# An order planner that lets VectorE's two-input operations run beside POOL's, and scalings of probabilities on POOL

## The chip, the cores and the metric

The kernel runs on one core of one Trainium2 chip. A core has a matrix engine (TensorE, PE in the profile; its weight loads are PEld), three engines for elementwise work (VectorE or DVE, ScalarE or ACT, GpSimd or POOL), and SyncE (SP), which issues all DMAs of this kernel. The matrix engine writes to an accumulator memory, PSUM; operands lie in SBUF. The metric is the device time of one execution in microseconds (us), the median of several runs.

## The reference

Windowed attention with a distance bias, followed by a gated feed-forward network (FFN), all in float32.

```python
# q, k, v: (8 batches, 8 heads, 576 tokens, 64)
scores = q @ k.T / 8 - slope[h] * (i - j)       # for 0 <= i - j < 128, else -1e9
attn   = exp(scores - max); attn = attn / (sum(attn) + 1e-9)
x      = (attn @ v), heads side by side         # (4608, 512)
out    = (sigmoid(x @ w_gate) * (x @ w_val)) @ w_out   # d_ff = 1536
```

The weights arrive as 64-bit floats and the output is float32.

## The kernel before

**Attention.** The 64 pairs of batch and head are worked as 32 units of two heads, each of nine blocks of 128 queries. PE makes the scores of eight blocks at a time (line 416); DVE copies masked halves over each other (428) and adds the bias and takes the row extreme (436); ACT takes the exponential and its row sum (439). Three blocks make a group: DVE adds 1e-9 to the three sums (454), takes the reciprocals (456), and each block is scaled by its reciprocal (`args` in `probabilities`, on ACT at line 459 or on DVE at 460). PE transposes the group (464), a copy brings it to SBUF (187 on ACT, 188 on DVE), and POOL writes it twice, masked, into the layout that the product with V needs (475). PE multiplies with V (501).

**First FFN part.** While the attention runs, PE also multiplies the finished tokens of the first 3072 with four of the twelve column blocks of the two weight matrices (553). Each float32 operand is split into a high part (a copy to a rounded type, lines 187 and 188) and a low part (the operand minus its high part, `minus`, lines 195 on POOL and 196 on DVE), and three products stand for one. Weights are turned from 64-bit to 32-bit floats by integer operations (`decode`, lines 312, 313 and 316).

**Second FFN part and the output.** The tokens lie in five groups. For each group seven combinations of its inputs are made (`add` in `ffn2`, line 650) and split; for every column block PE makes seven products (687), and DVE and ACT combine them and form the gate (694, 698, 702). The result goes to DRAM and comes back for the last product (817), again from seven combinations (`add` in `last`, line 772).

**What sets the order.** Nothing above is issued in the order in which the program states it. Each operation is put into a graph with an engine, a cost in us, its reads and writes, and a wanted time; some have further `ways`, on other engines with other costs. `Graph.order` plans all of it as a list: at each step it takes, over all operations whose inputs are planned and over all their ways, the one with the smallest start plus cost beyond the operation's cheapest way (plus 0.1 us for a way on DVE that isn't the first); ties go to the earlier wanted time. An operation starts when its engine is free, its inputs are there and, if the way counts as `shared`, when the one `port` is free; it then holds that port for its cost:

```python
s = max(free[e], o.ready, port if shared else 0.0)
key = (s + cost - least + (YIELD[e] if k else 0.0), o.want, o.seq)
...
if shared:
    port = o.start + o.cost
```

All POOL ways are shared; DVE's are where `port=True` or the third entry of a way says so. The instructions are then issued to each engine in the planned order, and semaphores keep them right whatever their real durations are. The plan thus sets two things: which engine does an operation that has several ways, and in which order each engine does its work.

Of the kernel before, what the change touches and what calls it, by code (L numbers as in the profile page):

```python
# [12 lines left out]
ALU = mybir.AluOpType  # L13
# [143 lines left out]
def dve_cost(n, psum=False, two=False):  # L157
    return 0.07 + n * (0.00104 if psum or two else 0.00053)
# [7 lines left out]
def attention_gated_ffn(ctx: ExitStack, tc: tile.TileContext, qd, kd, vd, wg, wv, wo, out):  # L166
    nc = tc.nc
    ctx.enter_context(tc.manual_schedule())
    g = Graph()
# [24 lines left out]
    def minus(out, a, b, n, reads, writes, want, psum=False, pool=True):  # L194
        way = ("POOL", 0.1 + n * 0.00223, True, lambda: nc.gpsimd.tensor_tensor(out(), a(), b(), op=ALU.subtract))
        g.add("DVE", dve_cost(n, psum, True), lambda: nc.vector.tensor_tensor(out(), a(), b(), op=ALU.subtract),  # L196
              reads, writes, want, port=not psum, ways=[way] if pool and not psum else [])

    ident = const.tile([P, P], F32, name="ident")
    make_identity(nc, ident)  # L200
# [102 lines left out]
    def decode(src, fc, bits, kb, want, release=0.0):  # L303
        s = raws[0] % NRAW
        raws[0] += 1
        kr = ("wraw", s)
        if src.dtype == F32:
            move(lambda: as32(bits()), lambda: src[fc], [], [kb], want, 256, False, release)
            return
        raw = lambda: T(moe, f"wraw{s}", [P, DM, 2], I32)  # L310
        move(lambda: raw().rearrange("p f t -> p (f t)"), lambda: src[fc].bitcast(I32), [], [kr], want, 512, True, release)
        g.add("ACT", act_cost(DM), lambda: nc.scalar.mul(as32(bits()), as32(raw()[:, :, 1]), 2.0 ** -112), [kr], [kb], want)
        g.add("DVE", dve_cost(DM), lambda: nc.vector.tensor_scalar(
            bits(), bits(), 3, None, op0=ALU.logical_shift_left), [], [kb], want, port=True)
        for word, scalar, o0 in ((0, 29, ALU.logical_shift_right), (1, -0x80000000, ALU.bitwise_and)):
            g.add("DVE", dve_cost(DM, two=True), lambda word=word, scalar=scalar, o0=o0: nc.vector.scalar_tensor_tensor(  # L316
                bits(), raw()[:, :, word], scalar, bits(), op0=o0, op1=ALU.bitwise_or), [kr], [kb], want, port=True)

    def parts(hi, lo, val, n, reads, k0, k1, want):
        copy(hi, val, n, reads, [k0], want)  # L320
# [127 lines left out]
    def probabilities(u, i0):  # L448
        m, _, st, pb, kst, kpb = three_of(u, i0)
        want = u.when(i0 + TRI)  # L450
        slack = 0.0 if u.n < HEAD else SLACK
        n, kb = TRI, ("both", m % NBOTH)
        both = lambda: spread2[m % NBOTH]
        g.add("DVE", 0.07, lambda: nc.vector.tensor_scalar_add(st()[:, 6:9], st()[:, 3:6], 1.0e-9),
              [(kst, 3 + e) for e in range(n)], [(kst, 6)], want)
        g.add("DVE", 0.09, lambda: nc.vector.reciprocal(st()[:, 6:9], st()[:, 6:9]), [], [(kst, 6)], want)
        for e in range(n):
            args = lambda e=e: (pb()[:, e], pb()[:, e], st()[:, 6 + e:7 + e])
            g.add("ACT", 0.3, lambda args=args: nc.scalar.mul(*args()), [(kst, 6)], [(kpb, e)], want,  # L459
                  ways=[("DVE", 0.16, True, lambda args=args: nc.vector.tensor_scalar_mul(*args()))])  # L460

        def transpose():
            for e in range(n):
                nc.tensor.transpose(tp[:, e], pb()[:, e], ident)  # L464

        g.add("PE", 0.11 * n + 0.1, transpose, [(kpb, e) for e in range(n)], [TP], want, slack=slack)
        copy(lambda: both(), lambda: tp[:, 0:n], n * P, [TP], [kb], want, psum=True)
        for own in range(2):
            step, cmp, mult = ([1, P], ALU.is_ge, -1) if own else ([-1, P], ALU.is_gt, 1)

            def spread(own=own, step=step, cmp=cmp, mult=mult):
                f0 = 2 * i0 + own
                nc.gpsimd.affine_select(pt(u)[:, f0:f0 + 2 * n - 1:2, :], both(), [[0, n], step], cmp, 0.0,  # L475
                                        base=0, channel_multiplier=mult)

            g.add("POOL", 0.13 + 0.12 * n, spread, [kb], [("pt", u.n % NPT, i0 + e, own) for e in range(n)], want)
# [155 lines left out]
    def ffn2(t, w, todo, F, ends=False):  # L634
# [13 lines left out]
        def add(o, a, b, op, reads, writes):  # L648
            way = ("POOL", 0.1 + m * 0.00223, True, lambda: nc.gpsimd.tensor_tensor(o(), a(), b(), op=op))
            g.add("DVE", dve_cost(m, two=True), lambda: nc.vector.tensor_tensor(o(), a(), b(), op=op), reads + ["w2pool"], writes, F,  # L650
                  port=True, ways=[way])

        if not made:
            for h in range(2):
                a = t0 + h * N2
                while a < t0 + (h + 1) * N2:
                    b = a // S
                    e = min((b + 1) * S, t0 + (h + 1) * N2)
# [3 lines left out]
                    a = e  # L662
# [12 lines left out]
        def chunk(i, fc):  # L675
            bx, by, bz = bank(), bank(), bank()
            e = turns[0] % (4 if ends else 2)
            turns[0] += 1
            a1, u2, p5, v5 = lambda: low()[:, 2], lambda: low()[:, 3], lambda: hs(e)[:, 1, 0:N2], lambda: hs(e)[:, 0, 0:N2]
            sg = [lambda h=h: T(moe, f"sg{h}", [P, NB], F32)[:, 0:N2] for h in range(2)]  # L680
            bk = lambda b: (lambda: mm[b][:, 0:N2])

            def product(k, b, start, wk):
                def six():
                    for c in range(2):
                        for j, (xp, wp) in enumerate(((0, 0), (0, 1), (1, 0))):
                            nc.tensor.matmul(mm[b][:, 0:N2], w.tile2(i, wp)[:, wk, c * P:(c + 1) * P], combo(k, xp, N2)[:, c],  # L687
                                             start=(start and c == 0 and j == 0), stop=(c == 1 and j == 2), skip_group_check=True)
                wa = 0 if wk < 2 else 2
                g.add("PE", 6 * (N2 / 2400 + 0.0133), six, [("ar", k, 0), ("ar", k, 1), ("w2", i, 0, wa), ("w2", i, 1, wa), "seam"],  # L690
                      [("mm", b)], 1.0e6)

            def total(o, b, a, reads, writes, okeys):
                g.add("DVE", dve_cost(N2, psum=True), lambda: nc.vector.tensor_tensor(o(), bk(b)(), a(), op=ALU.add),  # L694
                      [("mm", b), *reads] if okeys else reads, writes, F)

            def gate(b, h):
                g.add("ACT", act_cost(N2, psum=True), lambda: nc.scalar.activation(sg[h](), bk(b)(), AF.Tanh, scale=0.5),  # L698
                      [("mm", b)], [("sg", h)], F)

            def gated(o, val, reads, writes, h, psum):
                g.add("DVE", dve_cost(N2, psum, True), lambda: nc.vector.scalar_tensor_tensor(  # L702
                    o(), sg[h](), 1.0, val(), op0=ALU.add, op1=ALU.mult), [("sg", h), *reads], writes, F, port=not psum)

            ka, ku, kp, kv = "a1", "u2", ("hs", e, 1), ("hs", e, 0)
            product(0, bx, True, 0)
            copy(a1, bk(bx), N2, [("mm", bx)], [ka], F, psum=True)
            product(3, bz, True, 3)
            copy(p5, bk(bz), N2, [("mm", bz)], [kp], F, psum=True)
            product(4, bx, False, 4)  # L710
            copy(u2, bk(bx), N2, [("mm", bx)], [ku], F, psum=True)
            product(1, by, True, 1)
            total(bk(by), by, a1, [ka], [("mm", by)], False)
            gate(by, 0)
            product(5, bx, False, 5)
            total(p5, bx, p5, [], [kp], True)
            product(2, bz, False, 2)
            total(bk(bz), bz, u2, [ku], [("mm", bz)], False)
            gated(v5, bk(bz), [("mm", bz)], [kv], 0, True)
            product(6, bx, False, 6)  # L720
            gate(bx, 1)
            gated(p5, p5, [], [kp], 1, False)
            c, q, m = place(fc)
            move(lambda: hid[c, q, t][m].rearrange("p (h t) -> p h t", h=2), lambda: hs(e)[:, :, 0:N2], [kp, kv], [("hid", fc, t, 0)], F, N2, True)
# [32 lines left out]
    def last(t):  # L757
        F = FIRST + 2
        t0, N2 = GROUPS[t]
        n = 2 * N2  # L760
# [8 lines left out]

        def add(o, a, b, op, reads, writes):  # L770
            way = ("POOL", 0.1 + n * 0.00223, True, lambda: nc.gpsimd.tensor_tensor(o(), a(), b(), op=op))
            g.add("DVE", dve_cost(n, two=True), lambda: nc.vector.tensor_tensor(o(), a(), b(), op=op), reads, writes, F, port=True, ways=[way])

        bks = [[bank() for _ in range(3)] for _ in range(2)]
        bk = lambda b: (lambda: mm[b][:, 0:N2])
# [14 lines left out]
        for k in ORDER:  # L790
# [19 lines left out]
            for j in range(2):  # L810
                bx, by, bz = bks[j]
                b = {0: bx, 3: bz, 4: bx, 1: by, 5: bx, 2: bz, 6: bx}[k]
# [179 lines left out]
```

## Time and profile before

| | |
|---|---|
| median of 3 runs | 1001.75 us (999.0 to 1001.84) |
| the profiled execution | 1000.32 us, span 998.6 us |
| PE busy | 977.3 us (98%) |
| DVE busy | 771.5 us (77%) |
| ACT busy | 525.1 us (53%) |
| POOL busy | 124.5 us (12%), 217 instructions |

The span is the time from the first to the last instruction. A row of a group of instructions names the line, the engine, the operation, the tiles written and read, the shape and the count; then the busy time in us, the mean in ns, and the idle time just before with what ended it. A row of one line's instructions has least, median and most in ns. A row of a stretch begins with its bounds and length, then has the busy time of each engine (PE, PEld, DVE, ACT, POOL) with its count, and at the end the granted clock, the share of the DMA engines and GB/s; for one line's instructions it has only that line's engine.

### The profile page before, as it was taken

The page shows a single profiled execution, that of the slowest core. Times are in us where ns is not written, and L with a number is a line of the kernel's source. Part 1 is how long each engine was busy: PE and PEld are TensorE (multiplying, and loading weights), DVE is VectorE, ACT ScalarE, POOL GpSimd, SP SyncE. Part 2 cuts the span into 40 slices and gives each one's busy share as a digit, 9 for nine tenths or more (in the row PEclk, how much of TensorE's full clock was granted, in tenths as well). Part 3 has the DMA queues.
Part 4 walks back from the last instruction along what each step waited for, and adds up shares of the span by engine and source line. Part 5 has one row for each costly group of instructions (what it writes and reads, how often), then busy time and mean ns, then how long its engine had stood idle before and what let it go on. Part 6 is the DMA issues. An engine that isn't in the chain of part 4 may idle for free.

```text
span 998.6 us, 17735 instructions
## 1 busy us (share of the span) xinstructions
PE 977.3 (98%) x6202; PEld 843.6 (84%) x6202; DVE 771.5 (77%) x1951; ACT 525.1 (53%) x1350; POOL 124.5 (12%) x217
## 2 busy tenths in 40 slices
PE   8799899999999999999999999999999999999998
PEld 7577677778888999999988888888888888889998
DVE  7998968977866979966895596494479877878783
ACT  4999778768774546535354263362344433333341
POOL 1334543423331100000010000000000000000000
PEclk9899999999999999999999999999999999999999
DMA  7677866875724444332656265439885536162601
GB/s 271 219 259 251 325 225 219 293 233 181 235 93 169 145 148 132 132 137 90 221 203 233 113 209 223 169 116 366 282 307 156 184 99 208 58 194 80 190 16 64
DMA packets 82074, 185.98 MB, mean 186 GB/s; under 512 B 7744, under 2 KB 36800, under 8 KB 81984
## 3 DMA queue, kind: packets, MB, share of 16 engines
q1 hardware_dynamic: 81984, 184.84, 53.9%
q8 instruction: 49, 0.80, 0.3%
q14 instruction: 41, 0.34, 0.1%
HBM read 122.95 MB, written 61.87 MB: 185 GB/s over the span
## 4 chain that ended last, share of the span: by engine, by line
PE 87%; ACT 5%; DVE 5%; DMA 2%; issue 1%; POOL 0%; ACTq 0%; POOLq 0%; DVEq 0%
PE mm L687 39%; PE mm L817 25%; PE mm L553 10%; PE mm L501 5%; PE mm L416 4%; PE mm L464 3%; ACT pb L439 2%; DMA hid<-later_hs 1%; ACT pb L459 1%; PE mm L258 1%; DMA rows_h<-hid 1%; DVE mm L428 1%; ACT early_xr L187 1%; DVE wbits L316 0%; DMA kr<-in_k_dram 0%
## 5 line engine op out<-in xcount | busy, mean ns | idle before, releaser
L687 PE MATMUL mm<-xc,w2s 128*128 128x384 f32 (+1 forms) x2016 | 404.1, 362 | 0.1
L687 PEld LDWEIGHTS mm<-xc,w2s 128*128 128x128 f32 x2016 | 363.8, 188 | 40.3 <-DVE xc L196 0.5
L817 PE MATMUL mm<-duo,wo 128*128 128x512 f32 (+1 forms) x1260 | 259.2, 367 | 0.2 <-DVE duo L196 0.2
L817 PEld LDWEIGHTS mm<-duo,wo 128*128 128x128 f32 x1260 | 229.2, 188 | 30.2 <-DVE duo L196 0.6
L553 PE MATMUL mm<-first,first 128*128 128x512 f32 x576 | 156.1, 409 | 1.8 <-DVE first L196 1.8
L553 PEld LDWEIGHTS mm<-first,first 128*128 128x128 f32 x576 | 103.2, 191 | 25.0 <-issue 4.2
L694 DVE TENSOR_TENSOR mm<-mm,low 128x384 f32<-128x384 f32 (+1 forms) x96 | 60.3, 629 | 72.3 <-PE mm L687 72.1
L698 ACT ACTIVATE sg<-mm 128x384 f32<-128x384 f32 (+1 forms) x96 | 52.0, 544 | 117.9 <-PE mm L687 71.9
L439 ACT ACTIVATE pb<-pb,st 128x128 f32<-128x128 f32 x216 | 84.5, 397 | 8.4 <-DVE st L436 8.2
L187 ACT COPY low<-mm 128x512 f32<-128x512 f32 (+1 forms) x93 | 49.6, 534 | 71.3 <-PE mm L687 65.1
L501 PEld LDWEIGHTS mm<-pt,vr 128*64 128x64 f32 x832 | 61.4, 137 | 12.0 <-issue 8.6
L501 PE MATMUL mm<-pt,vr 128*64 128x256 f32 (+2 forms) x832 | 66.9, 306 | 0.0
L475 POOL TENSOR_SCALAR_AFFINE_SELECT pt<-early_h 128x384 f32<-128x384 f32 x96 | 53.1, 576 | 93.1 <-ACT early_h L187 90.7
L475 POOL TENSOR_SCALAR_AFFINE_SELECT pt<-early_xr 128x384 f32<-128x384 f32 x96 | 50.2, 546 | 100.7 <-ACT early_xr L187 91.3
L428 DVE COPY_PREDICATED mm<-early_h,mm 128x256 f32<-128x256 int32 (+1 forms) x144 | 48.8, 391 | 11.1 <-PE mm L416 10.7
L436 DVE CUSTOM_DVE_ANT_0 pb<-mm,early_h 128x128 f32<-128x128 f32 x216 | 51.0, 281 | 0.0
L464 PE MATMUL mm<-ident,pb 128*128 128x128 f32 x216 | 38.6, 287 | 11.2 <-ACT early_xr L187 7.2
L464 PEld LDWEIGHTS mm<-ident,pb 128*128 128x128 f32 x216 | 25.0, 142 | 23.9 <-ACT early_xr L187 9.7
L187 ACT COPY early_xr<-mm 128x384 f32<-128x384 f32 (+2 forms) x72 | 31.5, 460 | 21.1 <-PE mm L464 13.0
L439 ACT ACTIVATION_READ_ACCUMULATOR pb<-pb,st 128x1 f32 x216 | 41.8, 193 | 0.0
L694 DVE TENSOR_TENSOR later_hs<-mm,later_hs 128x384 f32<-128x384 f32 (+1 forms) x48 | 29.8, 620 | 14.2 <-PE mm L687 6.0
L702 DVE SCALAR_TENSOR_TENSOR later_hs<-sg,later_hs 128x384 f32<-128x384 f32 (+1 forms) x48 | 29.8, 621 | 12.5 <-ACT sg L698 12.5
(133 smaller groups left out, 1181.3 us busy)
## 6 DMA issues: line engine op xcount, KB each, us to landing
hid<-later_hs SPq DMA_DIRECT2D x24, 512.0 KB, 4.1
wo<-stash_o SPq DMA_DIRECT2D x12, 896.0 KB, 7.4
vr<-in_v_dram SPq DMA_DIRECT2D x32, 288.0 KB, 3.2
hid<-later_hs SPq DMA_DIRECT2D x24, 384.0 KB, 2.9
stash_o<-wtmp SPq DMA_DIRECT2D x12, 768.0 KB, 4.3
wraw<-in_moe_w_gate_dram SPq DMA_DIRECT2D x16, 512.0 KB, 4.9
wraw<-in_moe_w_val_dram SPq DMA_DIRECT2D x16, 512.0 KB, 4.7
kr<-in_k_dram SPq DMA_DIRECT2D x11, 576.0 KB, 6.0
```

Of the source, the lines that this page charges most:

```text
L187: g.add("ACT", act_cost(n, psum), lambda: nc.scalar.copy(out(), src()), reads, writes, want, release=release, ways=[("DVE", dve_cost(n, ps ...
L428: g.add("DVE", dve_cost((a1 - a0) * P, psum=True), lambda b=b, a0=a0, a1=a1: nc.vector.copy_predicated(quads(b)[:, a0:a1, 1:3], before[:, ...
L436: g.add("DVE", 0.21, lambda: nc.vector.tensor_tensor_reduce(pb()[:, e], sp[b][:, a, D:D + P], relm[u.p][:, w], op0=ALU.add, op1=ALU.min, s ...
L439: g.add("ACT", 0.39, lambda: nc.scalar.activation(pb()[:, e], pb()[:, e], AF.Exp, bias=st()[:, e:e + 1], scale=-1.0, accum_out=st()[:, 3 + ...
L464: nc.tensor.transpose(tp[:, e], pb()[:, e], ident)
L475: nc.gpsimd.affine_select(pt(u)[:, f0:f0 + 2 * n - 1:2, :], both(), [[0, n], step], cmp, 0.0, base=0, channel_multiplier=mult)
L501: nc.tensor.matmul(to()[e * D:(e + 1) * D, a - e * S - t0:b - e * S - t0], vraw(u)[:, c], seen, start=first, stop=last, skip_group_check=True)
L553: nc.tensor.matmul(mm[s][:, 0:wd], w.tile(kind, wi, i)[:, c * P:(c + 1) * P], xpart(x, c)[:, 0:wd], start=(k == 0 and c == 0), stop=(k == ...
L687: nc.tensor.matmul(mm[b][:, 0:N2], w.tile2(i, wp)[:, wk, c * P:(c + 1) * P], combo(k, xp, N2)[:, c], start=(start and c == 0 and j == 0), ...
L694: g.add("DVE", dve_cost(N2, psum=True), lambda: nc.vector.tensor_tensor(o(), bk(b)(), a(), op=ALU.add), [("mm", b), *reads] if okeys else ...
L698: g.add("ACT", act_cost(N2, psum=True), lambda: nc.scalar.activation(sg[h](), bk(b)(), AF.Tanh, scale=0.5), [("mm", b)], [("sg", h)], F)
L817: nc.tensor.matmul(mm[b][:, 0:N2], wo2(2 * q + m, wp)[:, k, j * P:(j + 1) * P], duo(xp)[:, m], start=(k in (0, 3, 1) and q == 0 and m == 0 ...
```

## The change

Operations of DVE with two inputs (`tensor_tensor`, `scalar_tensor_tensor`) lose their hold on the port in the plan: the subtractions of `minus`, the two integer merges of `decode`, the additions of `ffn2` and `last`, and the gate on SBUF operands. DVE's operations that keep it are the plain copies, the shift of `decode`, the scalings, and, newly, the addition of 1e-9. The scaling gets a third way, on POOL, as a multiplication by the reciprocal and then by 1.0. Two costs are set anew: 0.1 for 0.07 and 0.196 for 0.16 us.

```diff
     def minus(out, a, b, n, reads, writes, want, psum=False, pool=True):
         way = ("POOL", 0.1 + n * 0.00223, True, lambda: nc.gpsimd.tensor_tensor(out(), a(), b(), op=ALU.subtract))
         g.add("DVE", dve_cost(n, psum, True), lambda: nc.vector.tensor_tensor(out(), a(), b(), op=ALU.subtract),
-              reads, writes, want, port=not psum, ways=[way] if pool and not psum else [])
+              reads, writes, want, ways=[way] if pool and not psum else [])
...
             g.add("DVE", dve_cost(DM, two=True), lambda word=word, scalar=scalar, o0=o0: nc.vector.scalar_tensor_tensor(
-                bits(), raw()[:, :, word], scalar, bits(), op0=o0, op1=ALU.bitwise_or), [kr], [kb], want, port=True)
+                bits(), raw()[:, :, word], scalar, bits(), op0=o0, op1=ALU.bitwise_or), [kr], [kb], want)
...
-        g.add("DVE", 0.07, lambda: nc.vector.tensor_scalar_add(st()[:, 6:9], st()[:, 3:6], 1.0e-9),
-              [(kst, 3 + e) for e in range(n)], [(kst, 6)], want)
+        g.add("DVE", 0.1, lambda: nc.vector.tensor_scalar_add(st()[:, 6:9], st()[:, 3:6], 1.0e-9),
+              [(kst, 3 + e) for e in range(n)], [(kst, 6)], want, port=True)
...
             g.add("ACT", 0.3, lambda args=args: nc.scalar.mul(*args()), [(kst, 6)], [(kpb, e)], want,
-                  ways=[("DVE", 0.16, True, lambda args=args: nc.vector.tensor_scalar_mul(*args()))])
+                  ways=[("DVE", 0.196, True, lambda args=args: nc.vector.tensor_scalar_mul(*args())),
+                        ("POOL", 0.3, True, lambda args=args: nc.gpsimd.tensor_scalar(*args(), 1.0, op0=ALU.mult, op1=ALU.mult))])
...
             g.add("DVE", dve_cost(m, two=True), lambda: nc.vector.tensor_tensor(o(), a(), b(), op=op), reads + ["w2pool"], writes, F,
-                  port=True, ways=[way])
+                  ways=[way])
...
                 g.add("DVE", dve_cost(N2, psum, True), lambda: nc.vector.scalar_tensor_tensor(
-                    o(), sg[h](), 1.0, val(), op0=ALU.add, op1=ALU.mult), [("sg", h), *reads], writes, F, port=not psum)
+                    o(), sg[h](), 1.0, val(), op0=ALU.add, op1=ALU.mult), [("sg", h), *reads], writes, F)
...
-            g.add("DVE", dve_cost(n, two=True), lambda: nc.vector.tensor_tensor(o(), a(), b(), op=op), reads, writes, F, port=True, ways=[way])
+            g.add("DVE", dve_cost(n, two=True), lambda: nc.vector.tensor_tensor(o(), a(), b(), op=op), reads, writes, F, ways=[way])
```

## The prediction

> **What bounds the kernel now.** I read the page's slices first, then a table of engine time by stretch, then the chain of waits, and last the rows of the operations that the change touches. The page:
>
> ```profile
> span 998.6 us, 17735 instructions
> PE   8799899999999999999999999999999999999998
> DVE  7998968977866979966895596494479877878783
> ACT  4999778768774546535354263362344433333341
> POOL 1334543423331100000010000000000000000000
> ```
>
> Each digit is a slice of 25 us. PE is short of full only in the first five slices and the last; POOL is idle for most of the run. The table of stretches (length, then busy us of PE, weight load, DVE, ACT, POOL, each with its count) says how much:
>
> ```profile
> 0.00:20.00 20.00, 17.47 (x165) 15.14 (x169) 14.34 (x85) 9.90 (x39) 2.88 (x11) 1.00 0.79 281
> 20.00:120.00 100.00, 87.00 (x926) 66.79 (x919) 91.50 (x457) 89.42 (x351) 40.09 (x68) 0.96 0.75 254
> 120.00:320.00 200.00, 198.06 (x1793) 159.28 (x1793) 153.08 (x718) 144.36 (x526) 67.96 (x125) 0.99 0.62 208
> 340.00:600.00 260.00, 260.00 (x1375) 243.72 (x1374) 206.08 (x335) 121.45 (x215) 10.64 (x10) 1.00 0.47 165
> 600.00:998.60 398.60, 394.92 (x1859) 341.13 (x1857) 287.00 (x331) 148.41 (x203) 2.07 (x2) 1.00 0.50 169
> ```
>
> From 120 us on PE has work almost without a break: 1.94 us idle in 120 to 320, none in 340 to 600, 3.68 in the rest. Nothing that relieves DVE or ACT there can shorten the run. From 20 to 120 PE is idle 13.0 us while DVE is busy 91.5% and ACT 89.4%: there the two elementwise engines hold the attention back. The chain of waits, cut at 119 us, agrees:
>
> ```profile
> by line: ACT pb L439 17.0%; PE mm L501 10.2%; PE mm L553 7.1%; PE mm L416 6.7%; PE mm L464 6.1%; ACT pb L459 6.0%; DVE mm L428 5.4%; DVE wbits L316 4.1%; ACT early_xr L187 4.0%; ACT early_h L187 3.7%; issue 3.3%; ACT wbits L312 3.1%; DVE fi
> by line: PE mm L553 46.4%; PE mm L501 20.2%; PE mm L416 14.4%; PE mm L464 11.4%; DMA kr<-in_k_dram 2.5%; ACT pb L439 1.2%; ACT pb L459 0.7%; DVE first L196 0.7%; issue 0.6%; ACT tt L312 0.6%; ACT early_xr L187 0.5%; DVE tt L316 0.3%; ACT sg
> ```
>
> The first row is 20 to 119 us: PE's four lines hold 30.1%, issue 3.3%; with some 5% for what the cut row hides, about 62% lies with ACT and DVE. The second row is 119 to 318 us: PE holds 92%. So the change can gain in the front 100 us alone, and at most about the 13 us of idle PE there; and it can lose wherever a PE that is full now comes to wait.
>
> **Part 1: scalings may go to POOL.** There are 288 scalings (96 groups of three). By stretch, first on ACT (line 459), then on DVE (line 460):
>
> ```profile
> 20.00:120.00 100.00, 21.86 (x65) 0.96 0.75 254
> 20.00:120.00 100.00, 10.51 (x40) 0.96 0.75 254
> L475 POOL TENSOR_SCALAR_AFFINE_SELECT pt<-early_xr x96: 514/521/1207, 14.0 to 302.7; 128x384 f32<-128x384 f32 x96
> masks.py:199 POOL TENSOR_SCALAR_AFFINE_SELECT ident<-ident x1: 292/292/292, 1.1 to 1.1; 128x128 f32<-128x128 f32 x1
> L195 POOL TENSOR_TENSOR tt<-tt x8: 732/768/1597, 177.3 to 550.4; 128x256 f32<-128x256 f32 x8
> ```
>
> No scaling has run on POOL. Its nearest row is the mask of one 128x128 tile, 292 ns, also one input of the same size; I take 0.3 us. The other end is the shortest two-input operation, 732 ns for 256 elements.
>
> How many go there is the planner's choice. It takes the earliest of start plus cost beyond the cheapest way: 0.104 us for ACT and for POOL, 0.1 for DVE. An exponential on ACT has no such penalty, so on a busy ACT the exponentials go first and the scaling finds POOL, idle 60 of those 100 us. I take two thirds of the 105, 70 operations; the ends are none and all. Two thirds of 21.86 us is 14.6 off ACT, of 10.51 is 7.0 off DVE. The planner can shift copies between these two, so each gets 10.8 us less work; 62% of that is on the chain: **-6.7 us** (0 to -10). From 120 us on the same move is worth nothing, because PE's work covers it; were that cover gone, another 23.8 us on each engine would count.
>
> What stands behind a moved scaling: POOL works in order, so the mask operations (line 475) queue behind it, and the product with V waits for these. POOL's load there rises from 40.1 to about 61 us, so the queue is short and I add nothing; at the long end of 0.73 us it would be 91 us, and the gain of this part would be gone. No DMA is moved past anything: all DMAs are SP's, POOL issues none.
>
> **Part 2: subtractions and additions with two inputs in SBUF may be planned beside POOL.** In the old plan they hold the shared port, so POOL's own version is seldom the earlier one. Without that, it is chosen whenever DVE is booked further ahead than the difference in cost. In the front stretch line 196 has this much:
>
> ```profile
> 20.00:120.00 100.00, 10.86 (x17) 0.96 0.75 254
> ```
>
> A quarter moved is 2.7 us off DVE, half of it after the balance with ACT, 62% of that: **-0.8 us** (0 to -3).
>
> **Part 3: what POOL and DVE cost each other.** The plan now says nothing. The trace does not. Three pairs, first in the front, then twice in the later stages (start, us; the row of line 650 has ns, least, median and most):
>
> ```profile
> 110.22 2.92 POOL L195 TENSOR_TENSOR w2s<-tt,w2s 128x1280 fp32r<-128x1280 f32 x1
> 112.19 0.98 DVE L454 TENSOR_SCALAR st<-st 128x3 f32<-128x3 f32 x1
> 482.43 0.73 POOL L195 TENSOR_TENSOR tt<-tt 128x256 f32<-128x256 f32 x1 [139.19 <-DVE tt L196]
> 482.67 1.57 DVE L650 TENSOR_TENSOR low<-later_xr 128x1024 f32<-128x1024 f32 x1
> L650 DVE TENSOR_TENSOR later_xr<-later_xr x6: 946/1084/1220, 323.3 to 604.9; 128x768 f32<-128x768 f32 x3, 128x1024 f32<-128x1024 f32 x3
> 340.17 1.05 DVE L196 TENSOR_TENSOR w2s<-wbits,w2s 128x512 fp32r<-128x512 f32 x1
> 341.78 1.45 POOL L195 TENSOR_TENSOR tt<-wbits,tt 128x256 f32<-128x256 f32 x1
> ```
>
> The addition at 482.67 took 1.57 us; the longest of the same line and width in the row below it took 1.22. POOL's operation ended 0.49 us after the addition began (482.43 + 0.73 = 483.16), and 0.35 of that is in its time. POOL in turn took 1.45 instead of 0.73 us at 341.78. So a two-input operation of DVE and one of POOL do not overlap here: they take turns.
>
> The Trainium skill, page "SBUF — State Buffer", section "Who interferes with whom", states this rule: a DVE instruction with two SBUF inputs contends with a GpSimd instruction that reads SBUF, and the second to issue waits until the first has ended. The three pairs agree. By it, each of the 70 moved scalings can cost DVE its whole 0.3 us, and the sum at the end of this part would be +0.5 us in place of -3.8.
>
> How often does it strike? The mask operation's median is 521 ns, and the small DVE operation of line 454 gives the DVE side:
>
> ```profile
> L454 DVE TENSOR_SCALAR st<-st x96: 137/168/978, 10.9 to 292.5; 128x3 f32<-128x3 f32 x96
> L454 DVE TENSOR_SCALAR st<-st 128x3 f32<-128x3 f32 x96 | 20.4, 212 | 14.6 <-ACT pb L439 10.2 <-ACT early_xr L439 2.2 <-ACT early_h L439 1.8
> ```
>
> Mean less median is 44 ns, 4.2 us over 96 operations, or 0.02 us for each of some 210 operations of POOL. That is the low end, since the old plan kept the two apart; the high end is the whole 0.3. I take 0.1 us for each of 70: 7 us of DVE, 3.5 after the balance, 62% of it: **+2.2 us** (0.4 to 6.5). That line 454 itself is now planned apart from POOL can win back at most those 4.2 us over the run, a third of them in the front: under 0.5, taken as nothing, as are the two new cost figures for the planner.
>
> **Part 4: the later stages.** Between two token groups of the second FFN stage DVE must make the next inputs (lines 196 and 650), and there it is full:
>
> ```profile
> 330.00:430.00 100.00, 99.87 (x573) 99.01 (x572) 92.24 (x163) 51.78 (x96) 3.31 (x3) 1.00 0.43 143
> 500.00:530.00 30.00, 30.00 (x144) 26.03 (x143) 28.63 (x38) 17.25 (x26) 4.60 (x4) 1.00 0.68 246
> 650.00:670.00 20.00, 20.00 (x89) 16.54 (x89) 19.35 (x26) 14.11 (x21) 1.27 (x2) 1.00 0.20 72
> 747.00:998.60 251.60, 247.92 (x1211) 219.80 (x1210) 195.69 (x209) 90.25 (x113) 0.00 (x0) 1.00 0.40 127
> L687 PEld LDWEIGHTS mm<-xc,w2s 128*128 128x128 f32 x2016 | 363.8, 188 | 40.3 <-DVE xc L196 0.5
> ```
>
> PE already waited 0.5 us for such an input, so the slack is small. Where two or more such operations are queued, the new plan gives some to POOL. Two rows of POOL (732 ns for 256, 2.92 us for 1280) make 2.1 ns an element, so 2.4 us for 1024 elements, against 1.2 on DVE, and meanwhile DVE's other two-input work stands. I expect about 3 per handover, six handovers with the first; operations on PSUM fill most of the lost time. **+1.5 us** (-0.5 to +12, the upper end worked out under the third rival).
>
> **Sum:** -6.7 - 0.8 + 2.2 + 1.5 = **-3.8 us**. The profiled execution took 1000.32 us, 1.7 beyond its span, and would become 996.5. It lies 1.4 below the median of 1001.75; on the median's scale the forecast is **998 us**.
>
> **The rivals.** Three runs of this kernel spread over 0.28%, so 0.3% (3 us) is what a measurement can tell from no change.
>
> *The forecast, 998 us.* For it: DVE and ACT near 90% in the front and POOL idle beside them. Against: the pairs of part 3.
>
> *Nothing to be seen, about 1001 us.* POOL takes a third of the scalings (-3.3) and little else (-0.3), the collisions take 1.1 and the handovers 1.5 back: -1.0. The change then hardly does what it says, since the planner still holds POOL off while its own masks and DVE's copies have the port. For it: the old plan gave POOL few of the ways it had.
>
> *Everything at its good end, about 990 us.* All 105 scalings leave (-10), subtractions give -2, collisions cost 0.4: -11.6. Against: that is nearly all the idle PE in the front.
>
> *Slower, about 1009 us: POOL and DVE take turns at full price.* In the front 0.3 us per moved scaling leaves -6.7 - 0.8 + 6.5 = -1.0. At the handovers POOL takes a third of the two-input work. In the three stretches of part 4, line 196 (first three rows) and line 650 have:
>
> ```profile
> 330.00:430.00 100.00, 32.77 (x45) 1.00 0.43 143
> 500.00:530.00 30.00, 10.60 (x9) 1.00 0.68 246
> 650.00:670.00 20.00, 8.59 (x8) 1.00 0.20 72
> 330.00:430.00 100.00, 6.72 (x7) 1.00 0.43 143
> 500.00:530.00 30.00, 5.41 (x4) 1.00 0.68 246
> 650.00:670.00 20.00, 2.44 (x2) 1.00 0.20 72
> ```
>
> Together these are 39.5, 16.0 and 11.0 us; a third of it on POOL takes twice as long, which adds 13.2, 5.3 and 3.7 us where DVE has 7.8, 1.4 and 0.7 us of room: 12 us short, of which operations on PSUM hide about a third, leaving +8. Together +7. It decides once POOL gets about a quarter of the work there. For it: the 482.67 pair and the full DVE. Against: the old trace has the same rows of 92 to 98% busy DVE with PE never short by more than 0.5 us. The rule of the Trainium skill's page "SBUF — State Buffer", section "Who interferes with whom", speaks for this rival too.
>
> **How the numbers follow.** The forecast gets 0.42, the good end 0.08, nothing 0.28, slower 0.22. So faster by over 0.3% has 0.50, within it 0.28, slower 0.22. The forecast's own range is 993 to 1000. To hold 8 in 10 the range takes in most of both other sides: 988 to 1007.
>
> **What would show it.** Scalings on POOL: about 70 between 20 and 120 us, near 0.3 us each, with ACT and DVE both some 10 us lighter per unit of work, and the first product of the FFN (line 553) starting earlier than now. PE idle in 20 to 120 us falls below 13. Part 3: line 454's mean rises over 212 ns and two-input DVE groups rise over their medians. Part 4: rows of POOL at lines 195 of 768 or 1024 elements, and PE weight loads waiting for "xc" by more than a few us would be the slower rival. I am wrong if POOL's scalings take over 0.7 us, or if PE's idle time in the front stays while POOL does the scalings.

## The result and the profile after

The changed kernel takes 1024.85 us (median, 1024.53 to 1026.46) against 1001.32 us before: 1.0238 times as long, interval 1.0225 to 1.0251. The forecast was 998 us with a range up to 1007.

The page of the changed kernel (span, then PE, DVE, ACT and POOL in 40 slices):

```profile
span 1022.8 us, 17848 instructions
PE   8899999999998999999999999999998999999998
DVE  7998699967666979956795596494478887978783
ACT  5997668767675336534353353362334342323341
POOL 2777437545443401100040020030002301101000
```

PE's row looks as full as before, and DVE's too. POOL's row has filled up in the front as expected, and it has new spots in the later slices, up to 4 tenths. The stretches of the changed kernel (length, then busy us of PE, PEld, DVE, ACT, POOL with counts):

```profile
20.00:120.00 100.00, 88.98 (x926) 68.71 (x923) 90.16 (x415) 84.95 (x317) 67.65 (x116) 1.00 0.78 266
120.00:320.00 200.00, 196.64 (x1794) 157.22 (x1793) 148.68 (x700) 136.69 (x501) 93.50 (x173) 1.00 0.60 199
340.00:600.00 260.00, 254.61 (x1340) 236.63 (x1340) 201.79 (x307) 117.00 (x210) 40.41 (x25) 1.00 0.43 150
600.00:1022.80 422.80, 410.63 (x1916) 350.96 (x1914) 310.71 (x338) 149.62 (x209) 49.17 (x20) 1.00 0.50 169
```

From 340 us on PE is now idle 17.6 us where it was idle 3.7. When each part begins is read from the rows of its matmuls (after the count: least, median and most in ns, then first and last start in us). Of before:

```profile
L687 PE MATMUL mm<-xc,w2s x2016: 333/388/499, 331.6 to 735.4; 128*128 128x384 f32 x92, 128*128 128x512 f32 x92
L817 PE MATMUL mm<-duo,wo x1260: 333/389/496, 735.7 to 994.8; 128*128 128x512 f32 x108, 128*128 128x384 f32 x72
```

and of after:

```profile
L688 PE MATMUL mm<-xc,w2s x2016: 333/389/691, 327.9 to 753.5; 128*128 128x384 f32 x93, 128*128 128x512 f32 x91
L818 PE MATMUL mm<-duo,wo x1260: 333/389/501, 753.8 to 1019.0; 128*128 128x512 f32 x108, 128*128 128x384 f32 x72
```

The front, up to the first product of the second FFN part, is 3.7 us shorter (331.6 to 327.9). The second part, from there to the first product of the output, is 21.8 us longer (404.1 to 425.9). The output, from there to the end of the span, is 6.1 us longer (262.9 to 269.0). Together that is the 24.2 us by which the span grew. So the front won 3.7 of the 5.3 us that the forecast gave it, and the later stages lost over seven times as much.

What DVE and POOL did there shows in the timeline of the changed kernel, at the start of the output (start, us) and at the start of the second part:

```profile
760.32 2.40 POOL L195 TENSOR_TENSOR duo<-csum,duo 128x1024 fp32r<-128x1024 f32 x1 [74.42 <-ACT duo L187]
760.41 3.38 DVE L773 TENSOR_TENSOR csum<-rows_hs,rows_h 128x1024 f32<-128x1024 f32 x1 [4.12 <-DMA rows_h<-hid]
767.40 3.31 POOL L772 TENSOR_TENSOR csum<-csum,rows_xr 128x1024 f32<-128x1024 f32 x1 [4.69 <-DVE duo L196]
768.37 3.42 DVE L196 TENSOR_TENSOR duo<-csum,duo 128x1024 fp32r<-128x1024 f32 x1
```

```profile
327.19 3.12 POOL L195 TENSOR_TENSOR w2s<-tt,w2s 128x1280 fp32r<-128x1280 f32 x1 [1.38 <-ACT w2s L187]
327.46 3.67 DVE L651 TENSOR_TENSOR later_xr<-later_xr 128x768 f32<-128x768 f32 x1
331.65 0.94 DVE L196 TENSOR_TENSOR xc<-low,xc 128x768 fp32r<-128x768 f32 x1
332.65 0.47 PEld L688 LDWEIGHTS mm<-xc,w2s 128*128 128x128 f32 x3 [4.46 <-DVE xc L196]
```

DVE's addition at 760.41 started 0.09 us after POOL's subtraction and took 3.38 us: the 2.31 that POOL still needed and 1.07 of its own. At 327.46 an addition of 768 elements, 0.95 us before, took 3.67. Neither shares an operand with POOL's work of that moment. They ran one after the other. The last two rows show what that cost: PE's longest wait, 4.5 us, was for an operation that stood in DVE's queue behind the held one.

PE's waits of the changed kernel (what waited, for whom: us in total, times, longest):

```profile
PEld mm L688 <- DVE xc L196: 9.4, 7, 4.5
PEld mm L818 <- DVE duo L196: 6.7, 4, 2.1
PEld mm L688 <- DVE later_hs L695: 6.3, 9, 1.7
PEld mm L688 <- ACT low L187: 5.6, 7, 1.6
```

In the later stages PE waits for DVE and ACT; no row there names POOL. In the kernel before, the largest such row is 0.6 us. Two of the rows are inputs that come late (xc, duo). The other two (later_hs, low) are operations that read PSUM and free a bank for PE.

Waits are not the whole loss. Of the 21.8 us that the second part grew, 13.6 are PE idle (13.7 for 0.1) and 8.2 are PE busy for longer (412.2 for 404.0 us). Some of the latter is PE's clock. These are two stretches of 7 us of the changed kernel, soon after the 4.5 us wait:

```profile
333.00:340.00 7.00, 6.34 (x21) 5.84 (x20) 6.86 (x7) 2.64 (x4) 1.28 (x1) 0.51 0.41 128
341.00:348.00 7.00, 7.00 (x42) 7.00 (x41) 5.90 (x12) 2.24 (x6) 3.32 (x3) 1.00 0.58 191
```

At a granted clock of 0.51 PE got through 21 products where it did 42 at 1.00. Seven us at half the clock are worth about 3.4 us (an estimate from these rows). The kernel before has no such stretch in these stages. That the wait brought the clock down was not tested by itself, and where the other 5 us or so of longer busy time come from stays open.

### The profile page after: what moved, and what is told of

Its sections match the earlier page's. It is cut to its first block, busy times and chain, and to the rows that moved or that the text cites. A ratio compares the mean times of both kernels' runs of the same rounds, so it can differ in the third digit from the quotient of the medians.

```text
span 1022.8 us, 17848 instructions
## 1 busy us (share of the span) xinstructions
PE 983.4 (96%) x6208; PEld 841.2 (82%) x6208; DVE 786.1 (77%) x1873; ACT 509.3 (50%) x1292; POOL 262.7 (26%) x353
## 4 chain that ended last, share of the span: by engine, by line
PE 69%; DVE 19%; ACT 5%; issue 3%; DMA 2%; POOL 1%; ACTq 0%; DVEq 0%; POOLq 0%; SPq 0%
PE mm L688 29%; PE mm L818 23%; PE mm L554 7%; PE mm L502 4%; PE mm L416 3%; DVE xc L196 2%; PE mm L465 2%; ACT pb L439 2%; DVE wbits L316 2%; DVE later_hs L703 1%; DVE mm L428 1%; DVE w2s L196 1%; DVE tt L316 1%; DVE mm L695 1%; DVE duo L196 1%
## 5 line engine op out<-in xcount | busy, mean ns | idle before, releaser
L688 PE MATMUL mm<-xc,w2s 128*128 128x384 f32 (+1 forms) x2016 | 412.3, 365 | 13.8 <-DVE xc L196 6.9
L554 PE MATMUL mm<-first,first 128*128 128x512 f32 x576 | 153.5, 405 | 0.3 <-ACT pb L459 0.3
L554 PEld LDWEIGHTS mm<-first,first 128*128 128x128 f32 x576 | 102.0, 188 | 23.5 <-issue 3.3
L187 ACT COPY low<-mm 128x384 f32<-128x384 f32 (+1 forms) x94 | 49.9, 533 | 64.7 <-PE mm L688 63.4
L502 PEld LDWEIGHTS mm<-pt,vr 128*64 128x64 f32 x832 | 61.0, 137 | 13.6 <-issue 7.7
L502 PE MATMUL mm<-pt,vr 128*64 128x256 f32 (+3 forms) x832 | 68.2, 307 | 0.8 <-ACT early_h L187 0.8
L476 POOL TENSOR_SCALAR_AFFINE_SELECT pt<-early_xr 128x384 f32<-128x384 f32 x96 | 54.9, 596 | 51.5 <-ACT early_xr L187 38.4
L461 POOL TENSOR_SCALAR pb<-pb,st 128x128 f32<-128x128 f32 x84 | 43.5, 530 | 25.9 <-DVE st L456 21.6
L703 DVE SCALAR_TENSOR_TENSOR later_hs<-sg,later_hs 128x384 f32<-128x384 f32 (+1 forms) x48 | 32.2, 671 | 12.0 <-ACT sg L699 11.9
```

What stands on the lines that cost most here:

```text
L187: g.add("ACT", act_cost(n, psum), lambda: nc.scalar.copy(out(), src()), reads, writes, want, release=release, ways=[("DVE", dve_cost(n, ps ...
L502: nc.tensor.matmul(to()[e * D:(e + 1) * D, a - e * S - t0:b - e * S - t0], vraw(u)[:, c], seen, start=first, stop=last, skip_group_check=True)
L554: nc.tensor.matmul(mm[s][:, 0:wd], w.tile(kind, wi, i)[:, c * P:(c + 1) * P], xpart(x, c)[:, 0:wd], start=(k == 0 and c == 0), stop=(k == ...
```

## The experiments

Two theories were set against each other. **T, turns:** two-input operations of POOL and DVE exclude each other; POOL's wide operations hold up DVE, DVE's queue is in order, and PE waits for what stands in it. **O, order:** without the port the plan puts DVE's own work in a worse order. Later a third was added, **D, delay:** POOL's wide operations are slow, and PE waits for their results.

For every kernel, from the same rows of its one profiled execution: start of the second part, its length, and the length of the output, in us. The ratio is to the kernel before, which was run again beside each group (medians 1000.64 to 1000.98).

| kernel | median | ratio (95% interval) | start | second part | output |
|---|---|---|---|---|---|
| before | 1001.32 | | 331.6 | 404.1 | 262.9 |
| changed | 1024.85 | 1.0238 (1.0225 to 1.0251) | 327.9 | 425.9 | 269.0 |
| ports_only | 1025.12 | 1.0239 (1.0199 to 1.0279) | 324.4 | 428.4 | 269.0 |
| scale_only | 997.46 | 0.9954 (0.9937 to 0.9971) | 326.7 | 406.3 | 262.7 |
| scale_375 | 1000.54 | 1.0001 (0.9986 to 1.0015) | 327.1 | 407.2 | 263.4 |
| no_wide | 1005.62 | 1.0048 (1.0035 to 1.0060) | 330.9 | 409.6 | 263.1 |
| late_port | 1006.92 | 1.0058 (1.0039 to 1.0077) | 329.4 | 413.2 | 263.4 |
| no_sub | 997.75 | 0.9968 (0.9957 to 0.9979) | 327.5 | 405.4 | 262.6 |
| early_ports | 996.38 | 0.9959 (0.9944 to 0.9974) | 326.5 | 406.6 | 262.5 |
| early_noscale | 1002.00 | 1.0012 (1.0001 to 1.0023) | 332.6 | 404.8 | 264.6 |
| extra_two | 1049.77 | 1.0500 (1.0476 to 1.0525) | 330.0 | 454.8 | 262.8 |
| extra_set | 1007.76 | 1.0071 (1.0055 to 1.0086) | 330.9 | 411.9 | 263.8 |
| clean_two | 1018.35 | 1.0183 (1.0157 to 1.0210) | 328.0 | 427.8 | 263.5 |
| clean_set | 999.00 | 0.9993 (0.9980 to 1.0005) | 328.4 | 407.1 | 262.4 |

### The two halves of the change

The first takes the scaling's way on POOL out of the changed kernel; the second puts that way into the kernel before and leaves all ports.

```diff
# ports_only, against the changed kernel
-                  ways=[("DVE", 0.196, True, ...tensor_scalar_mul(*args())),
-                        ("POOL", 0.3, True, ...)])
+                  ways=[("DVE", 0.196, True, ...tensor_scalar_mul(*args()))])
```

```diff
# scale_only, against the kernel before
-                  ways=[("DVE", 0.16, True, ...tensor_scalar_mul(*args()))])
+                  ways=[("DVE", 0.196, True, ...tensor_scalar_mul(*args())),
+                        ("POOL", 0.3, True, ...tensor_scalar(*args(), 1.0, op0=ALU.mult, op1=ALU.mult))])
```

> The changed kernel without POOL's way for the scalings. T: the later loss stays and the front's gain is gone: 1022 to 1030 us. Rival S: if the late and long scalings were behind the loss, about 1001.

> The kernel before with POOL's way for the scalings and the new cost on DVE, all ports as before. T, with the forecast's front part: the scalings alone carry the front's gain, 996 to 999 us. Rival S: the scalings take 0.53 us on POOL in place of the planned 0.3 and gain nothing, and what the front won came from the narrow subtractions: 1000 to 1003 us.

The halves have opposite signs. The ports alone make the whole loss (1.0239); the scalings alone make the kernel faster (0.9954), close to what the forecast had for both together. Rival S, that late scalings cause the loss, is out. Of the two, only the ports' loss is as large as the change's; the scalings' 3 us are in it and cannot be seen.

### Which operations, or which order?

```diff
# no_wide, against the changed kernel
-              reads, writes, want, ways=[way] if pool and not psum else [])
+              reads, writes, want, ways=[way] if pool and not psum and n < 768 else [])
...
-                  ways=[way])     # add in ffn2 and in last
+                  )
```

> The changed kernel, but operations of 768 elements and more (the seven combinations of lines 651 and 773 and the low parts of that width) have no way on POOL; the port in the plan stays as the change set it. Theory T (turns): POOL's 24 wide two-input operations and DVE's two-input operations take turns, and this makes PE wait in the two later stages, which lost 21.8 and 6.1 us. Then this kernel keeps the 3.7 us that the front won and loses little later: 996 to 1001 us. Rival O (order): what costs is the new order of DVE's own queue, since the port no longer spaces its work. Then most of the loss stays: 1012 us or more.

```diff
# late_port, against the changed kernel
-              reads, writes, want, ways=[way] if pool and not psum else [])
+              reads, writes, want, port=not psum if n in (768, 1024) else None, ways=...)
...
+                  port=True,      # add in ffn2 and in last; port=not psum in gated
```

> The changed kernel with the port given back to the wide operations alone (additions and low parts of 768 and 1024 elements, and the gate); the attention is planned as in the changed kernel. T: 996 to 1000 us, with no or very few wide operations on POOL. O: also about 996 to 1000, since the order of the later stages is then nearly the old one. If instead the loss comes from the front (weights or tokens that are handed over later), it stays over 1010.

Without the 24 wide operations on POOL (and two subtractions of 1280 elements, one of them the row at 327.19 above), 19 of 23.5 us are back, so the missing port alone does not explain the bulk. But T's own number was missed: 1005.6, not up to 1001. The same holds for late_port (1006.9, not up to 1000), whose plan still put three operations of 768 elements on POOL. In both the excess is in the second part (409.6 and 413.2 for 404.1). What POOL still did there in no_wide, by its groups from 325 to 760 us:

```profile
L195 POOL TENSOR_TENSOR tt<-tt 128x256 f32<-128x256 f32 x8 | 8.5, 1071 | 9.6 <-DVE tt L196 9.3
L195 POOL TENSOR_TENSOR tt<-tt,wbits 128x256 f32<-128x256 f32 x7 | 7.8, 1117 | 39.1 <-DVE tt L316 39.1
L195 POOL TENSOR_TENSOR w2s<-wbits,w2s 128x512 fp32r<-128x512 f32 x4 | 6.9, 1715 | 56.7 <-DVE mm L694 41.6 <-ACT w2s L187 15.1
L195 POOL TENSOR_TENSOR wg<-wbits,wg 128x256 fp32r<-128x256 f32 x6 | 6.8, 1142 | 219.7 <-ACT wg L187 219.7
```

These are subtractions of the weights, 256 elements in 1.07 to 1.14 us where an undisturbed one takes 0.73: they collide too. The next kernel takes them away as well, and another gives the port back to all that belongs to the later stages (there the merges, the additions and the gate hold it as in the kernel before).

```diff
# no_sub, against the changed kernel
-              reads, writes, want, ways=[way] if pool and not psum else [])
+              reads, writes, want)
...
-                  ways=[way])     # add in ffn2 and in last
+                  )
```

> The changed kernel with no subtraction or addition on POOL at all; POOL has the masks and the scalings. The kernel without the wide ones still lost 5 us, all of it in the second FFN part (409.3 us for 403.8). Theory T (turns): these are the narrow operations of 256 and 512 elements that POOL does there while DVE is full; without them 995 to 999 us, the second FFN part at 404 to 406. Rival O (order of DVE's queue without the port): 1003 to 1007, the second FFN part at 409.

> The changed kernel with the port given back to all that belongs to the second FFN part and the output (its weights, combinations and gate), so that only the first FFN part's weights and tokens are planned free of the port; scalings on POOL as changed. T: 995 to 999 us. If the front's two gains (4.9 us with the scalings alone, 7.2 with the ports alone, both up to the first product of the second FFN part) add up: 990 to 994. O: also 995 to 999.

```diff
# early_ports, against the changed kernel: late=False only for decode and parts of the first FFN part
-    def minus(out, a, b, n, reads, writes, want, psum=False, pool=True):
+    def minus(out, a, b, n, reads, writes, want, psum=False, pool=True, late=True):
...
-              reads, writes, want, ways=[way] if pool and not psum else [])
+              reads, writes, want, port=late and not psum, ways=[way] if pool and not psum else [])
```

no_sub speaks for T and against O. Its plan is as free of the port as the changed kernel's, but no subtraction or addition runs on POOL. It takes 997.75 us and its second part 405.4. So the missing port alone does not cost these 27 us. It is not yet the last word on O: every plan is made anew, and DVE's order in no_sub is not that of the changed kernel. The pair at the end of the next section has one and the same order. early_ports is as fast; the front's two earlier starts did not add up to the 990 to 994 that was possible.

### The collision by itself

T says that POOL's work costs even when nobody needs it. Two kernels add such work to the kernel before: beside 24 of DVE's low parts POOL subtracts from the identity matrix, or, in the second, mostly sets it to zero for about as long. The extra work is issued from within DVE's operation and the planner does not know of it. In the traces, DVE, ACT, PE and POOL do the rest in exactly the order of the kernel before.

```diff
# extra_two, against the kernel before; clean_two has the same on no_sub
         def work():
+            beside(b, n)          # only for combinations 1, 5, 2 and 6 of a new group
             nc.vector.tensor_tensor(out(), a(), b(), op=ALU.subtract)
...
+        def beside(b, n):
+            for x in range(n // P):
+                nc.gpsimd.tensor_tensor(ident, ident, b()[:, x % 2, x // 2 * 64:x // 2 * 64 + P], op=ALU.subtract)
```

```diff
# extra_set, and clean_set on no_sub
+            nc.gpsimd.tensor_tensor(ident, ident, b()[:, 0, 0:P], op=ALU.subtract)
+            for x in range(2 * (n // P - 1)):
+                nc.gpsimd.memset(ident, 0.0)
```

> The kernel before; beside 24 low parts of the second FFN part (combinations 1, 5, 2 and 6 of each new group), which DVE computes as before, POOL starts on extra work that nobody waits for: 6 or 8 subtractions of 128 elements, with two inputs from SBUF, into the identity matrix, which is no longer needed by then. T: POOL and DVE take turns, DVE's rows at lines 196 and 650 grow and PE waits: 1006 us or more. Rival D (delay): a wide operation on POOL costs only because PE waits for its own, later result; then the extra work costs nothing: 1000 to 1003.

> As the kernel with extra subtractions, but POOL's extra work is one subtraction of 128 elements (which starts it at the same time) and then 10 or 14 memsets of 128 elements, about as long. T, with the Trainium skill's rule (page SBUF - State Buffer, section Who interferes with whom: a GpSimd instruction that only writes does not contend with two-input ones): 1000 to 1003 us. If any work on POOL slows DVE, or POOL's own late subtractions behind the extra work are what costs: as slow as the other.

Both were slower, by 49 and 7 us, but neither was clean: the kernel before has a few subtractions of its own on POOL in these stages, and they stood in the queue behind the extra work. In extra_two:

```profile
ACT wtmp L187 <- POOL tt L195: 18.1, 2, 9.1
DVE w2s L188 <- POOL tt L195: 8.3, 1, 8.3
ACT wbits L317 <- POOL tt L195: 7.4, 1, 7.4
```

So the pair was run again on no_sub, where nothing in these stages waits for POOL. The order of all other operations is again exactly that of no_sub, on all four engines.

> The kernel without any subtraction or addition on POOL (997.75 us), so that in the later stages nothing of the program waits for POOL, plus the extra work on POOL that nobody waits for: beside 24 low parts of the second FFN part, 6 or 8 subtractions of 128 elements with two inputs from SBUF. Theory T (turns): DVE's two-input rows grow by some 10 to 20 us in all and PE waits: 1002 to 1015 us. Rival D (delay: wide operations on POOL cost only through those that wait for their result): 996 to 999.

> The same with memsets in place of the extra subtractions but the first. T, with the rule of the Trainium skill (page SBUF - State Buffer, section Who interferes with whom) that work of GpSimd that only writes does not hold up two-input operations: 996 to 1000 us. If any work on POOL holds up DVE: as slow as the other.

The extra subtractions cost 20.6 us against no_sub (997.75 to 1018.35, above the 1015 expected), the memsets 1.3, about what the measurement can tell. D is refuted as an explanation of a cost of this size: work that nobody waits for does the harm. O is out for it too, since the order is the same in all three kernels. The groups of POOL's extra work, first in clean_two, then in clean_set:

```profile
L653 POOL TENSOR_TENSOR ident<-ident,xc 128x128 f32<-128x128 f32 x168 | 139.4, 830 | 250.7 <-ACT xc L187 238.0
```

```profile
L654 POOL MEMSET ident<- 128x128 f32 x288 | 61.6, 214 | 16.6
L652 POOL TENSOR_TENSOR ident<-ident,xc 128x128 f32<-128x128 f32 x24 | 21.0, 877 | 267.4 <-ACT xc L187 266.1
```

A subtraction of 128 elements took 830 ns on average, 452 at the least (the rows of its line), while a memset took 214 of 204. And PE's waits in clean_two:

```profile
PEld mm L696 <- DVE later_hs L703: 15.3, 11, 3.3
PE mm L696 <- DVE later_hs L703: 11.3, 10, 2.9
PEld mm L696 <- DVE xc L199: 4.3, 6, 2.0
```

Here PE waits most for line 703 (694 in the kernel before): the addition of a PSUM bank to an SBUF tile, which frees the bank. With one SBUF input it did not collide with POOL: it took 618 ns on average, against 620 in no_sub. It is late because two-input operations ahead of it in DVE's queue are held: the durations of DVE's operations, compared one by one, add up to 23.8 us more than in no_sub. As in the changed kernel, part of the cost is PE's clock, which fell to 0.50 in three stretches of some 3 us (from 331, 536 and 696 us); clean_set has none in these stages.

The page "SBUF — State Buffer" of the Trainium skill, section "Who interferes with whom", says that a two-input instruction of DVE contends with a GpSimd instruction that reads SBUF and not with one that only writes it. Both halves agree with this pair of kernels, 20.6 us against 1.3.

### Is it the scalings that gain, and does their planned cost matter?

```diff
# early_noscale, against early_ports
-                  ways=[("DVE", 0.196, True, ...),
-                        ("POOL", 0.3, True, ...)])
+                  ways=[("DVE", 0.196, True, ...)])
# scale_375, against scale_only
-                        ("POOL", 0.3, True, ...)])
+                        ("POOL", 0.375, True, ...)])
```

> Only the first FFN part's weights and tokens planned free of the port, all later operations holding it, and no scaling on POOL. If the front's gain needs the scalings (ACT and DVE relieved): 1000 to 1003 us. If free ports alone carry a gain in the front, as the earlier start of the second FFN part with ports alone (324.4 for 331.6 us) suggests: 996 to 999.

> The kernel before with the scalings also on POOL, at the planned cost that an undisturbed one takes (0.375 us) in place of 0.3. If the plan gains by the true cost: 993 to 997 us. If the cost only moves a few scalings back: 996 to 999, as with 0.3 (997.5).

Without scalings on POOL, early_ports falls from 996.4 to 1002.0: the gain is the scalings'. The truer cost is no better: it takes their count from 84 to 52, and the ratio is 1.0001 where it was 0.9954, outside both of its expectations. Its second part starts as early (327.1 for 326.7), and its profiled execution is 2.0 us longer; why that plan loses it again was not followed further.

## Why the prediction was wrong

**What bounds the kernel: right.** The gain can only come from the front, and anything that makes PE wait later costs in full. In none of the 14 kernels is the second part shorter than 404.1 us or the output shorter than 262.4.

**Part 1, scalings (-6.7 us): right mechanism, too large.** POOL took 100 scalings, 44 of them from 20 to 120 us, not 70. The rows of that stretch in the changed kernel, for the scalings on ACT, DVE and POOL:

```profile
20.00:120.00 100.00, 11.39 (x33) 1.00 0.78 266
20.00:120.00 100.00, 8.14 (x28) 1.00 0.78 266
20.00:120.00 100.00, 21.22 (x44) 1.00 0.78 266
L461 POOL TENSOR_SCALAR pb<-pb,st x84: 369/376/1352, 16.1 to 303.9; 128x128 f32<-128x128 f32 x84
```

ACT lost 10.5 us of scalings and DVE 2.4, for 14.6 and 7.0 in the forecast. The median scaling of the row took 0.376 us on POOL, near the 0.3 that was taken; the mean of its 84 is 0.53. PE's idle time there fell from 13.0 to 11.0 us, and the first product of the FFN (line 553) starts at 35.1 us instead of 51.0. With the scalings alone (scale_only) the second part starts 4.9 us earlier, where this part had 6.7.

**Part 2, subtractions in the front (-0.8), and part 3, collisions in the front (+2.2): near in sum, not shown term by term.** Parts 1 to 3 together were to give -5.3; the second part starts 3.7 us earlier. But the terms do not add up as the forecast took them to: with the scalings alone it starts 4.9 us earlier, with the ports alone 7.2, with both 3.7. So the nearness of the sum is in part luck. The collisions show in DVE's groups:

```profile
L454 DVE TENSOR_SCALAR st<-st 128x3 f32<-128x3 f32 x96 | 20.2, 213 | 21.2 <-ACT pb L439 11.3 <-ACT early_xr L439 5.2 <-ACT early_h L439 4.3
L316 DVE SCALAR_TENSOR_TENSOR wbits<-wraw,wbits 128x512 int32<-128x512 int32 x52 | 38.7, 746 | 0.2
```

The merges of line 316 went from 684 to 746 ns. Line 454 stayed at 213 ns, so planning it apart from POOL won nothing, as was taken.

Two of the three pairs shown in part 3 are not pairs of two-input operations at one time. Line 454 has one input. DVE's row at 340.17 ended at 341.22, before POOL's at 341.78 began; what ran beside the latter was this one:

```profile
341.61 1.03 DVE L650 TENSOR_TENSOR low<-later_xr 128x768 f32<-128x768 f32 x1
```

It ended 0.86 us after POOL's operation began, which with 0.73 us of POOL's own makes 1.59; 1.45 was measured. So the conclusion stands, but on two pairs instead of three.

**Part 4, the later stages (+1.5, at most +12): the step that failed.** It measured +27.9: 21.8 in the second part and 6.1 in the output. Three things in it were wrong. First, "operations on PSUM fill most of the lost time": they can't, since DVE works in order, so they stand behind the held operation, and they are what frees PE's banks. Second, the sum has no term for the output, whose row shows DVE's room as a mean (195.69 of 251.6 us busy); 4.3 of the 5.0 us by which PE's idle time grew there fall in its first 25 us, where the first inputs have no lead. Third, the rival that named the mechanism asked for a quarter or a third of the wide work on POOL; 11 of 66 operations in the second part and 13 of 165 in the output were enough for most of it. The sum also has nothing for collisions of the narrow subtractions of weights: taking these off POOL too was worth another 7.9 us (no_wide to no_sub), 4.2 of them in the second part. These are two groups of the output on DVE, before:

```profile
L196 DVE TENSOR_TENSOR duo<-rows_xr,duo 128x1024 fp32r<-128x1024 f32 (+1 forms) x20 | 21.9, 1113 | 0.5
L772 DVE TENSOR_TENSOR csum<-rows_hs,rows_h 128x1024 f32<-128x1024 f32 (+1 forms) x5 | 5.6, 1120 | 7.0 <-DMA rows_h<-hid 6.9
```

and after:

```profile
L196 DVE TENSOR_TENSOR duo<-rows_xr,duo 128x1024 fp32r<-128x1024 f32 (+1 forms) x20 | 35.1, 1769 | 0.6
L773 DVE TENSOR_TENSOR csum<-rows_hs,rows_h 128x1024 f32<-128x1024 f32 (+1 forms) x5 | 8.4, 1689 | 6.9 <-DMA rows_h<-hid 6.9
```

The same 25 operations took 16 us more, for 13 that POOL took over in that stage, worth some 15 us on DVE at 1.1 to 1.2 us each. So handing work to POOL did not lighten DVE there: from the output's first product to the end of the span DVE was busy for 211.5 us, before for 202.6.

**The rival that came true** was "slower: POOL and DVE take turns at full price", with 0.22 and +7 us. Its mechanism is shown by no_sub and by clean_two against clean_set; its price was less than a third of the true one (+8 for the later stages, where it was +27.9), for the same reasons as part 4. The trace of before held the decisive evidence: the pairs at 482.43 and 341.78 show the exclusion. I used them for an average cost per operation where the question was what stands behind the held one.

**What stays open.** The front's earlier start follows no one rule: ports_only starts the second part earliest (324.4) without any scaling on POOL, and early_noscale, with free ports in the first FFN part alone, starts it at 332.6. The plan's order changes throughout with each such edit, and which part of it did this was not separated.

Of the versions that beat both kernels, scale_only (0.9954), early_ports (0.9959) and no_sub (0.9968) cannot be told apart, since their intervals overlap; scale_only needs the smallest edit, the new way alone.

## What to carry to other kernels

Before a planner or a hand-made order lets two engines overlap, look in the trace for one pair that did run at the same time: a long operation that ended just after the other engine's shows exclusion at once. Price such a collision by the queue behind the held operation, not by its mean over the stage; in an in-order queue even operations that cannot collide are late. And split a change that bundles a new choice (scalings on POOL) with a loosened rule (no port), since here one gained 0.5% and the other lost 2.4%.

## What the runs showed of the hardware

Two-input operations on POOL and DVE took turns in every pair looked at, to within 0.15 us: 3.38 us for a 1.1 us addition that began 0.09 us after a POOL subtraction of 2.40. The same holds in POOL's direction: 0.83 us on average for subtractions that take 0.45 at the least. Memsets on POOL, 288 of them in the busiest stages, cost 1.3 us, and 24 subtractions went with them. After a wait of 4.5 us PE's granted clock was 0.51 for 7 us. A multiplication by a value per partition and then by a constant, 128x128, took 0.376 us on POOL at the median.
